# Attention and a gated causal convolution on one core: the depthwise convolution in quarter-array matmuls

## The chip, the cores and the metric

The kernel runs on one core of a Trainium2 chip. A core has five engines that run their own instruction streams and wait for one another by semaphores: TensorE (PE, matmuls and transposes, with a separate row PEld for weight loads), VectorE (DVE), ScalarE (ACT), GpSimd (POOL) and SyncE (SP, which here only issues DMAs). A name with a q behind it, such as SPq, is an engine's issuing side. Matmuls write to PSUM, which has eight banks; everything else works in SBUF. The metric is the device time of one execution in microseconds (us). Three runs of the kernel before took 227.63, 227.98 and 228.9 us; the median is 227.98.

## The reference

```python
# q, k, v: (8, 8, 576, 64): batch, heads, sequence, head width
scores = matmul(q, k.T) / sqrt(64)
scores = where(row // 64 >= col // 64, scores, -1e9)       # causal by blocks of 64
attn   = exp(scores - max); attn = attn / (sum(attn) + 1e-9)
x      = matmul(attn, v) -> (8, 576, 512)                  # heads side by side
# w_val, w_out: (512, 512); conv_w: (5, 512)
gate_pre = sum over k of conv_w[k] * (x shifted down by 4 - k rows)
gate     = 1 / (1 + exp(-gate_pre))
out      = ((gate * (x @ w_val)) @ w_out)                  # (8, 576, 512), float32
```

All 512 features of the convolution are independent: each has its own five weights, and no feature mixes with another. The multiplication by `w_val` and `w_out` mixes them.

## The kernel before

The work is cut into 32 pairs of heads: pair `p` is batch `b = p // 4` and feature chunk `g = p % 4`, 128 features. One loop over `p` (with 12 iterations more to drain it) writes the instructions of all engines in the order in which they run; no scheduler changes it. Each engine takes its own instructions in that order. One iteration `p` issues, on PE:

1. `s_tile(p, 0)` and `s_tile(p, 1)`: score matmuls. The two heads of a pair lie on the partitions 0 to 63 and 64 to 127, so these matmuls use 64 rows of the array and 128 columns (`64*128` in the profile). ACT takes the exponentials from PSUM (`pt`), POOL zeroes the masked corners.
2. `av(p - 1)`: 30 matmuls of the pair before, with 65 columns streamed (64 values and a column of ones for the sum). DVE divides by the sum (`rc`, `x`).
3. `s_tile(p, 2)`.
4. `conv(p - 2)`: the convolution of one feature chunk. For every tap `kk` there is a diagonal 128x128 matrix `DG[:, g, kk, :]` with the tap's weights, and the chunk of `x`, features on partitions, is streamed through it at an offset of `kk` columns. Five taps add up in PSUM, once for each half of the 576 rows (`hf`): ten matmuls of 288 columns. ACT then takes `tanh` of half the sum (`th`), for sigmoid(z) = (1 + tanh(z / 2)) / 2.
5. `trans(p + 2)`: eight transposes of the queries and keys that are needed two iterations later, and every fourth iteration four more for the last 64 rows (`trans_tails`, "tails" below). POOL has cast them to 16 bits before.
6. `s_tile(p, 3)`: two small score matmuls.
7. `val(p - 5)`: 128 output features of `x @ w_val`, two halves of four matmuls of 288 columns; DVE multiplies by `th + 1` and writes `gv` (`w_val` was scaled by 0.5 when it was cast).
8. `xtrans(p - 1)`: five transposes of the attention's result into `xts`, features on partitions.
9. `out_tile`: in most later iterations one, at times two: four matmuls of 512 columns with `gv` as weights and `w_out` streamed. DVE copies the result out and SP stores it.

All but the scores use four PSUM banks, `G0` to `G3`, in turn: `g1()` takes the next, `g2()` the next two. A step waits until whoever read its bank last is done: DVE for most, ACT for the banks of `conv`. With no tails an iteration takes nine banks, so `val`'s second half gets the first bank of `conv`, and `xtrans` the second.

SP issues the loads of `q`, `k` (four iterations ahead) and `v` (three ahead) and the stores in one queue, in program order. ACT issues the loads of the weights at the start. `weights(s)` in iterations 0 to 5 prepares them: the loads and the transposed taps `convT` in 0, the diagonals `DG` on DVE in 1 (20 operations), the casts of `w_val` on ACT in 2 and 3 and of `w_out` in 4 and 5.

All matmuls that are no transposes are issued by the helper `mm` at L33, so the profile shows them under that line; they are told apart by the tiles: `G<-xt,DG` is the convolution, `G<-v,pt` the attention's second product, `G<-xt,w_val` the projection, `G<-w_out,gv` the output.

Of the kernel before, what the change touches and what calls it, by code (L numbers as in the profile page):

```python
# [10 lines left out]
def kernel(  # L11
# [10 lines left out]
    nc = tc.nc  # L22
    fp32 = mybir.dt.float32
    fp16 = mybir.dt.float16
# [31 lines left out]
    convT = const([128, 4, 5], fp32, "convT")  # L56
    DG = const([128, 4, 5, 128], fp16, "DG")

# [176 lines left out]

    def conv(p):
        b, g = divmod(p, 4)
        r = g2()
        for hf in range(2):
            for kk in range(5):  # L240
                mm(G[0:128, (r + hf) % 4, 0:288], DG[0:128, g, kk, 0:128],
                   xts[b % NX][0:128, g, kk + 288 * hf:kk + 288 * hf + 288],
                   start=(kk == 0), stop=(kk == 4))
        t = p4.tile([128, 2, 288], fp32, tag="th", name="th")
        th[p] = t
        for hf in range(2):
            nc.scalar.activation(out=t[0:128, hf, 0:288], in_=G[0:128, (r + hf) % 4, 0:288],  # L247
                                 func=AF.Tanh, bias=0.0, scale=0.5)

    def val(p):  # L250
        b, g = divmod(p, 4)
        r = g2()
        for hf in range(2):
            for fc in range(4):
                mm(G[0:128, (r + hf) % 4, 0:288], w_val_sb[0:128, fc, 128 * g:128 * g + 128],
                   xts[b % NX][0:128, fc, 4 + 288 * hf:4 + 288 * hf + 288],
                   start=(fc == 0), stop=(fc == 3))
# [3 lines left out]
        t = th.pop(p)  # L261
        for hf in range(2):
            nc.vector.scalar_tensor_tensor(  # L263
                out=gv[u][0:128, g, bi, hf, 0:288], in0=t[0:128, hf, 0:288], scalar=1.0,
                in1=G[0:128, (r + hf) % 4, 0:288], op0=ALU.add, op1=ALU.mult)

# [43 lines left out]
    def weights(s):  # L310
        if s == 0:
            nc.scalar.dma_start(out=w_st[0:128],
                                in_=moe_w_val.rearrange("(fc p) n -> p fc n", p=128))
            nc.scalar.dma_start(out=w_st2[0:128],
                                in_=moe_w_out.rearrange("(fc p) n -> p fc n", p=128))
            r = g1()
# [6 lines left out]
        elif s == 1:  # L323
            for g in range(4):
                for kk in range(5):
                    nc.vector.tensor_scalar(out=DG[0:128, g, kk, 0:128], in0=ident16[0:128],
                                            scalar1=convT[0:128, g, kk:kk + 1], scalar2=None,
                                            op0=ALU.mult)
        elif s in (2, 3):
            a = 2 * (s - 2)  # L330
            nc.scalar.activation(out=w_val_sb[0:128, a:a + 2, 0:512],
                                 in_=w_st[0:128, a:a + 2, 0:512],
                                 func=AF.Copy, bias=0.0, scale=0.5)
        elif s in (4, 5):
            a = 2 * (s - 4)
            nc.scalar.activation(out=w_out_sb[0:128, a:a + 2, 0:512],
                                 in_=w_st2[0:128, a:a + 2, 0:512],
                                 func=AF.Copy, bias=0.0, scale=1.0)

    outs = []  # L340
    for p in range(NP + 12):
# [13 lines left out]
        if p < NP:  # L355
# [16 lines left out]
        if 0 <= p - 5 < NP:  # L372
            val(p - 5)
        if 0 <= p - 1 < NP:
# [41 lines left out]
```

## Time and profile before

| what | us |
|---|---|
| median of three runs | 227.98 |
| the profiled execution, as timed | 228.03 |
| its span, first to last instruction | 226.2 |
| PE busy | 206.6 |
| PEld busy | 148.1 |
| DVE busy | 136.0 |
| ACT busy | 124.7 |
| POOL busy | 84.7 |
| convolution matmuls, 320 of 287 ns | 44.9 busy |
| tanh, 64 of 437 ns | 23.7 busy |
| projection matmuls, 256 of 287 ns | 36.6 busy |

Times in the profile are us from the start of the span unless marked ns. A matmul's record runs from its start to a modelled end, and the next may start long before that; so a group's busy time is the union of its records, and the pace of PE is seen from starts, not from the mean length. In a row of a timeline the first number is the start, the second the length of the merged stretch, and the count stands behind the x; what stands in brackets is the engine's idle time before it and what ended it. The mean granted clock of PE was 0.985 of full speed.

### The profile page before, as it was taken

The page shows a single profiled execution, that of the slowest core. Times are in us where ns is not written, and L with a number is a line of the kernel's source. Part 1 is how long each engine was busy: PE and PEld are TensorE (multiplying, and loading weights), DVE is VectorE, ACT ScalarE, POOL GpSimd, SP SyncE. Part 2 cuts the span into 40 slices and gives each one's busy share as a digit, 9 for nine tenths or more (in the row PEclk, how much of TensorE's full clock was granted, in tenths as well). Part 3 has the DMA queues.
Part 4 walks back from the last instruction along what each step waited for, and adds up shares of the span by engine and source line. Part 5 has one row for each costly group of instructions (what it writes and reads, how often), then busy time and mean ns, then how long its engine had stood idle before and what let it go on. Part 6 is the DMA issues. An engine that isn't in the chain of part 4 may idle for free.

```text
span 226.2 us, 6996 instructions
## 1 busy us (share of the span) xinstructions
PE 206.6 (91%) x2712; PEld 148.1 (65%) x2712; DVE 136.0 (60%) x326; ACT 124.7 (55%) x197; POOL 84.7 (37%) x224
## 2 busy tenths in 40 slices
PE   0494599999999999999999999999999999999993
PEld 0363387777777776677777776776777776767661
DVE  1228245556666766666666667666666666656683
ACT  2055189977755554566666554555666665563100
POOL 1380465454534343544434333544454332220000
PEclk9999589999999999999999999999999999999999
DMA  5999997978888968987689767977888762111226
GB/s 131 214 235 330 199 203 169 206 154 187 187 193 207 228 147 205 245 200 190 164 187 227 175 173 173 231 188 188 198 194 206 174 159 96 46 49 46 96 93 232
DMA packets 120715, 40.32 MB, mean 178 GB/s; under 512 B 115045, under 2 KB 115045, under 8 KB 120682
## 3 DMA queue, kind: packets, MB, share of 16 engines
q1 hardware_dynamic: 119616, 37.77, 69.4%
q10 hardware_dynamic: 1066, 2.11, 2.8%
q8 instruction: 21, 0.34, 0.7%
q14 instruction: 12, 0.10, 0.2%
HBM read 30.42 MB, written 9.44 MB: 176 GB/s over the span
## 4 chain that ended last, share of the span: by engine, by line
PE 83%; SPq 5%; DMA 4%; ACT 2%; issue 2%; DVE 1%; POOL 0%; POOLq 0%; DVEq 0%; ACTq 0%
PE G L33 60%; PE S L33 13%; PE G L155 6%; DMA qkst<-in_k_dram 4%; PE G L228 4%; SPq L107 3%; ACT pt L186 1%; SPq L115 1%; PE G L142 1%; ACT th L247 1%; SPq L118 1%; POOL qk L131 0%; DVE rc L218 0%; SPq L96 0%; DVE osb L274 0%
## 5 line engine op out<-in xcount | busy, mean ns | idle before, releaser
L186 ACT ACTIVATE pt<-S 128x1024 f16<-128x1024 f32 (+1 forms) x128 | 101.1, 841 | 80.3 <-PE S L33 79.4
L160 DVE COPY qkT<-G 128x1024 f16<-128x1024 f16 x32 | 22.1, 692 | 45.2 <-PE G L155 45.2
L193 POOL MEMSET pt<- 64x128 f16 x96 | 17.2, 199 | 74.3 <-ACT pt L186 73.8
L33 PE MATMUL G<-xt,DG 128*128 128x288 f16 x320 | 44.9, 287 | 0.0
L131 POOL CAST qk<-qkst 128x1024 f16<-128x1024 f32 x31 | 32.4, 1045 | 21.3 <-DMA qkst<-in_k_dram 19.0
L33 PEld LDWEIGHTS <-pt 128*128 128x128 f16 x960 | 32.4, 99 | 7.2 <-issue 6.5
L33 PE MATMUL G<-xt,w_val 128*128 128x288 f16 x256 | 36.6, 287 | 0.0
L33 PE MATMUL G<-v,pt 128*128 128x65 f16 x960 | 36.2, 197 | 0.0
L33 PE MATMUL G<-w_out,gv 128*128 128x512 f16 x144 | 35.5, 379 | 0.0
L33 PEld LDWEIGHTS <-DG 128*128 128x128 f16 x320 | 28.6, 97 | 8.5
L155 PE MATMUL G<-ident,qk 128*128 128x128 f16 x256 | 21.2, 230 | 14.0 <-POOL qk L131 8.1
L263 DVE SCALAR_TENSOR_TENSOR gv<-th,G 128x288 f16<-128x288 f32 x64 | 29.0, 454 | 6.7 <-PE G L33 4.7
L219 DVE TENSOR_TENSOR x<-G,rc 128x320 f16<-128x320 f32 x64 | 31.5, 492 | 2.2
L274 DVE COPY osb<-G 128x512 f32<-128x512 f32 x36 | 24.9, 692 | 10.5 <-PE G L33 10.4
L33 PE MATMUL S<-qkT 64*128 64x512 f16 (+3 forms) x256 | 30.5, 313 | 0.8 <-ACT pt L186 0.6
L155 PEld LDWEIGHTS <-qk 128*128 128x128 f16 x256 | 17.9, 103 | 16.0 <-POOL qk L131 8.6
L33 PEld LDWEIGHTS <-qkT 64*128 64x128 f16 x512 | 16.4, 96 | 18.2 <-issue 12.4
L247 ACT ACTIVATE th<-G 128x288 f32<-128x288 f32 x64 | 23.7, 437 | 6.7 <-PE G L33 6.7
L33 PEld LDWEIGHTS <-w_val 128*128 128x128 f16 x256 | 22.8, 98 | 6.3
L134 POOL CAST v<-vst 128x640 f16<-128x640 f32 x32 | 23.2, 725 | 2.2 <-POOL pt L195 0.3
L218 DVE RECIPROCAL rc<-G 128x5 f32<-128x5 f32 x64 | 12.2, 190 | 15.2 <-PE G L33 14.3
L33 PEld LDWEIGHTS <-gv 128*128 128x128 f16 x144 | 13.0, 98 | 10.7
(33 smaller groups left out, 96.8 us busy)
## 6 DMA issues: line engine op xcount, KB each, us to landing
out_dram<-osb SPq DMA_DIRECT2D x36, 256.0 KB, 2.2
qkst<-in_q_dram SPq DMA_DIRECT2D x64, 128.0 KB, 3.0
qkst<-in_k_dram SPq DMA_DIRECT2D x64, 128.0 KB, 3.2
vst<-in_v_dram SPq DMA_DIRECT2D x64, 128.0 KB, 3.3
tlst<-in_q_dram SPq DMA_DIRECT2D x8, 128.0 KB, 3.5
tlst<-in_k_dram SPq DMA_DIRECT2D x8, 128.0 KB, 4.1
vst<-in_v_dram SPq DMA_DIRECT2D x32, 32.0 KB, 2.7
w_st<-in_moe_w_val_dram ACTq DMA_DIRECT2D x1, 1024.0 KB, 6.0
```

Of the source, the lines that this page charges most:

```text
L33: nc.tensor.matmul(out=out, lhsT=lhsT, rhs=rhs, start=start, stop=stop, skip_group_check=True)
L131: eng.tensor_copy(out=t[0:128], in_=s[0:128])
L134: nc.gpsimd.tensor_copy(out=v16s[p % NV][0:128, 0:5, 0:2, 0:64], in_=vsts[p % NVS][0:128, 0:5, 0:2, 0:64])
L155: nc.tensor.transpose(out=r[:, o:o + 128], in_=t[0:128, i, c, 0:2, 0:64], identity=ident16[0:128, 0:128])
L160: nc.vector.tensor_copy(out=o[0:128], in_=r.rearrange("p (i s) -> p i s", i=2))
L186: nc.scalar.activation(out=pts[p % NPT][0:128, 0:2, 512 * t:512 * t + n], in_=s[0:128, 0:2, 0:n], func=AF.Exp, bias=0.0, scale=0.125)
L193: nc.gpsimd.memset(pt[64:128, 0:2, o:o + 64], 0.0)
L218: nc.vector.reciprocal(out=rc[0:128], in_=O[:, :, 64:65])
L219: nc.vector.tensor_tensor(out=x[0:128, 0:5, h, 0:64], in0=O[:, :, 0:64], in1=rc[0:128].to_broadcast([128, 5, 64]), op=ALU.mult)
L247: nc.scalar.activation(out=t[0:128, hf, 0:288], in_=G[0:128, (r + hf) % 4, 0:288], func=AF.Tanh, bias=0.0, scale=0.5)
L263: nc.vector.scalar_tensor_tensor(out=gv[u][0:128, g, bi, hf, 0:288], in0=t[0:128, hf, 0:288], scalar=1.0, in1=G[0:128, (r + hf) % 4, 0:288 ...
L274: nc.vector.tensor_copy(out=o[0:128], in_=G[0:128, r, 0:512])
```

## The change

The convolution is computed in quarters of the array. A unit is now two feature chunks (`c2`: chunks 0 and 1, or 2 and 3) and one half of the rows (`hf`), where it was one chunk and both halves. A chunk's 128 features lie on two halves of the partitions (`row` 0 and 1). For every tap four matmuls of 64x64 are issued: chunk `2 * c2 + col`, feature half `row`, each with the 64x64 diagonal block of its features, since the rest of the diagonal matrix is zero. The result of (`row`, `col`) goes to bank `row` of the unit's two and to the partitions of `col`. A unit has 20 matmuls of 288 columns, in the order (0,0), (1,1), (0,1), (1,0) within a tap, and there are 32 units as before; each unit still gives two banks to two `tanh` operations.

So the features come out in another order: the 128 partitions of a result hold one half of each of two chunks. To match, the columns of `w_val` are permuted when they are cast (four ACT operations of half the size instead of two), and the rows of `w_out` when they are loaded (four DMAs of 64 partitions instead of one of 128). The diagonals `DG` hold only 64 columns, and DVE makes them in 40 operations of 64x64. Since a unit needs two chunks, it is issued one iteration later: `p - 3` instead of `p - 2`; iterations 3 to 34 hold one each, where 2 to 33 did.

```diff
-    DG = const([128, 4, 5, 128], fp16, "DG")
+    DG = const([128, 4, 5, 64], fp16, "DG")
...
-    def conv(p):
-        b, g = divmod(p, 4)
+    def conv(b, c2, hf):
         r = g2()
-        for hf in range(2):
-            for kk in range(5):
-                mm(G[0:128, (r + hf) % 4, 0:288], DG[0:128, g, kk, 0:128],
-                   xts[b % NX][0:128, g, kk + 288 * hf:kk + 288 * hf + 288],
+        t = th.get((b, c2))
+        if t is None:
+            t = th[(b, c2)] = p4.tile([128, 2, 2, 288], fp32, tag="th", name="th")
+        for kk in range(5):
+            for rc in ((0, 0), (1, 1), (0, 1), (1, 0)):
+                row, col = rc
+                g = 2 * c2 + col
+                rs, cs = slice(64 * row, 64 * row + 64), slice(64 * col, 64 * col + 64)
+                mm(GT[(r + row) % 4][cs, 0:288], DG[rs, g, kk, 0:64],
+                   xts[b % NX][rs, g, kk + 288 * hf:kk + 288 * hf + 288],
                    start=(kk == 0), stop=(kk == 4))
-        for hf in range(2):
-            nc.scalar.activation(out=t[0:128, hf, 0:288], in_=G[0:128, (r + hf) % 4, 0:288],
+        for row in range(2):
+            nc.scalar.activation(out=t[0:128, row, hf, 0:288],
+                                 in_=GT[(r + row) % 4][0:128, 0:288],
                                  func=AF.Tanh, bias=0.0, scale=0.5)
...
-    def val(p):
-        b, g = divmod(p, 4)
+    def val(b, x):
+        c2, row = divmod(x, 2)
...
-            nc.scalar.dma_start(out=w_st2[0:128],
-                                in_=moe_w_out.rearrange("(fc p) n -> p fc n", p=128))
+            for col in range(2):
+                for x in range(2):
+                    nc.scalar.dma_start(
+                        out=w_st2[64 * col:64 * col + 64].rearrange(
+                            "p (a x) n -> p a x n", a=2)[:, :, x],
+                        in_=moe_w_out.rearrange("(a c x i) n -> c x i a n",
+                                                a=2, c=2, x=2)[col, x])
...
-                    nc.vector.tensor_scalar(out=DG[0:128, g, kk, 0:128], in0=ident16[0:128],
-                                            scalar1=convT[0:128, g, kk:kk + 1], scalar2=None,
-                                            op0=ALU.mult)
+                    for hh in range(2):
+                        hs = slice(64 * hh, 64 * hh + 64)
+                        nc.vector.tensor_scalar(out=DG[hs, g, kk, 0:64],
+                                                in0=ident16[hs, 64 * hh:64 * hh + 64],
+                                                scalar1=convT[hs, g, kk:kk + 1], scalar2=None,
+                                                op0=ALU.mult)
         elif s in (2, 3):
             a = 2 * (s - 2)
-            nc.scalar.activation(out=w_val_sb[0:128, a:a + 2, 0:512],
-                                 in_=w_st[0:128, a:a + 2, 0:512],
-                                 func=AF.Copy, bias=0.0, scale=0.5)
+            for x in (a, a + 1):
+                nc.scalar.activation(
+                    out=w_val_sb[0:128, 0:4, 128 * x:128 * x + 128].rearrange(
+                        "p f (c i) -> p f c i", c=2),
+                    in_=w_st[0:128].rearrange("p f (a c r i) -> p f a r c i",
+                                              a=2, c=2, r=2)[:, :, x // 2, x % 2],
+                    func=AF.Copy, bias=0.0, scale=0.5)
...
-        if 0 <= p - 2 < NP:
-            conv(p - 2)
+        if 0 <= p - 3 < NP:
+            bq, un = divmod(p - 3, 4)
+            conv(bq, un // 2, un % 2)
...
-            val(p - 5)
+            val(*divmod(p - 5, 4))
```

On PE, in the middle of the loop, where the convolution stands between the third score tile and the transposes of `q` and `k`, the kernel before has this order (`qkT` and `kt` are transposed queries and keys, `qk16` those to be transposed, G0 to G3 the four banks):

```order
L33 LDWEIGHTS qkT_2062
L33 MATMUL S_2276<-kt_0_99,qkT_2062 128x64
L33 LDWEIGHTS DG_86
L33 MATMUL G3_107<-xt_0_101,DG_86 128x288 [waits DVE_49]
L33 LDWEIGHTS DG_86
L33 MATMUL G3_107<-xt_0_101,DG_86 128x288
...
L33 MATMUL G0_104<-xt_0_101,DG_86 128x288 [waits DVE_49]
...
L155 LDWEIGHTS qk16_2166 [waits Pool_49]
L155 MATMUL G1_105<-ident16_79,qk16_2166 128x128 [waits DVE_49]
```

And the changed kernel, at the same place:

```order
L33 LDWEIGHTS qkT_1925
L33 MATMUL S_2151<-kt_1_100,qkT_1925 128x64
L33 LDWEIGHTS DG_86
L33 MATMUL G3_107<-xt_0_101,DG_86 64x288 [waits DVE_49]
L33 LDWEIGHTS DG_86
L33 MATMUL G0_104<-xt_0_101,DG_86 64x288 [waits DVE_49]
L33 LDWEIGHTS DG_86
L33 MATMUL G3_107<-xt_0_101,DG_86 64x288
...
L155 LDWEIGHTS qk16_2027 [waits Pool_49]
L155 MATMUL G1_105<-ident16_79,qk16_2027 128x128 [waits DVE_49]
```

The block lies between the same neighbours. It alternates between its two banks at every matmul, where it filled one after the other, and both are complete only at its end.

On ACT, in the first iterations, the difference is this (`w_st_83` is where the weights `w_out` land, `pt` the exponentials):

```order
 L186 ACTIVATE pt_96<-S 128x2x512 x2
-L312 DMA w_st<-in_moe_w_val_dram 128x4x512
-L314 DMA w_st_83<-in_moe_w_out_dram 128x4x512
+L319 DMA w_st<-in_moe_w_val_dram 128x4x512
+L323 DMA w_st_83<-in_moe_w_out_dram 64x2x512 x4
 L186 ACTIVATE pt_96<-S 128x2x512
```

```order
 L186 ACTIVATE pt_98<-S 128x2x512 x2
-L331 ACTIVATE w_val<-w_st 128x1024
+L347 ACTIVATE w_val<-w_st 128x4x128 x2
 L186 ACTIVATE pt_98<-S 128x2x512
-L247 ACTIVATE th<-G_107 128x288
-L247 ACTIVATE th<-G_104 128x288
 L186 ACTIVATE pt_98<-S 128x2x64
```

Three DMA issues more stand ahead of the third exponential of iteration 0; in iteration 2 the cast of `w_val` is two operations, and the pair of `tanh` has moved to the next iteration.

More of the change, by code (lines that the diff above doesn't have):

```diff
@@ L254, in val @@
             for fc in range(4):
[L255 removed]
+                mm(GT[(r + hf) % 4][0:128, 0:288],
+                   w_val_sb[0:128, fc, 128 * x:128 * x + 128],
                    xts[b % NX][0:128, fc, 4 + 288 * hf:4 + 288 * hf + 288],
@@ L260, in val @@
             gv[u] = p2.tile([128, 4, 2, 2, 288], fp16, tag="gv", name="gv")
-        t = th.pop(p)
+        t = th[(b, c2)]
         for hf in range(2):
             nc.vector.scalar_tensor_tensor(
-                out=gv[u][0:128, g, bi, hf, 0:288], in0=t[0:128, hf, 0:288], scalar=1.0,
-                in1=G[0:128, (r + hf) % 4, 0:288], op0=ALU.add, op1=ALU.mult)
+                out=gv[u][0:128, x, bi, hf, 0:288], in0=t[0:128, row, hf, 0:288], scalar=1.0,
+                in1=GT[(r + hf) % 4][0:128, 0:288], op0=ALU.add, op1=ALU.mult)
+        if row == 1:
+            th.pop((b, c2))
     def out_tile(u, t):
```

2 lines of the change are left out of this document (removed).

## The prediction

> **What bounds the kernel now.** First the page: busy time, the slices, and the chain that ended last.
>
> ```profile
> span 226.2 us, 6996 instructions
> PE 206.6 (91%) x2712; PEld 148.1 (65%) x2712; DVE 136.0 (60%) x326; ACT 124.7 (55%) x197; POOL 84.7 (37%) x224
> PE   0494599999999999999999999999999999999993
> PE 83%; SPq 5%; DMA 4%; ACT 2%; issue 2%; DVE 1%; POOL 0%; POOLq 0%; DVEq 0%; ACTq 0%
> ```
>
> PE has gaps in the first six slices and hardly any after; 83% of the chain is PE. Matmuls are pipelined, so a busy PE alone proves little. I therefore read the windows, cut at the starts of loop iterations (each begins with the first score matmul): one iteration in the middle, the start-up iterations 2 to 5, the long stretch of iterations 6 to 28, and one with much DMA.
>
> ```profile
> 101.84:107.89 6.05, 6.05 (x86) 4.35 (x85) 3.94 (x9) 3.74 (x6) 2.45 (x6) 1.00 0.79 191
> 27.21:47.29 20.08, 19.55 (x298) 14.84 (x298) 10.49 (x27) 18.27 (x28) 10.51 (x25) 0.94 0.92 190
> 47.29:188.92 141.63, 141.39 (x1940) 102.00 (x1939) 92.84 (x215) 86.02 (x138) 60.78 (x145) 1.00 0.79 189
> 119.98:126.26 6.28, 6.28 (x90) 4.57 (x89) 4.21 (x10) 3.74 (x6) 2.45 (x6) 1.00 0.96 230
> ```
>
> The columns are length, then busy PE, PEld, DVE, ACT and POOL, the clock, the DMA share and GB/s. PE fills the long stretch at full clock, ACT and DVE have some 2 us free in each 6.05 us. Next, PE's order inside that iteration; here the **starts** matter, since a record's length includes its pipeline's end.
>
> ```profile
> 101.84 0.61 PE L33 MATMUL S<-qkT 64*128 64x512 f16 x6
> 102.38 1.09 PE L33 MATMUL G<-v,pt 128*128 128x65 f16 x30
> 103.40 0.28 PE L33 MATMUL S<-qkT 64*128 64x256 f16 x2
> 103.52 0.29 PE L33 MATMUL S<-kt,qkT 64*128 64x64 f16 x8
> 103.74 1.40 PE L33 MATMUL G<-xt,DG 128*128 128x288 f16 x10
> 104.98 0.61 PE L155 MATMUL G<-ident,qk 128*128 128x128 f16 x8
> 105.52 0.20 PE L33 MATMUL S<-kt 64*128 64x64 f16 x2
> 105.66 1.15 PE L33 MATMUL G<-xt,w_val 128*128 128x288 f16 x8
> 106.65 0.44 PE L228 MATMUL G<-ident,x 128*128 128x128 f16 x5
> 106.93 1.03 PE L33 MATMUL G<-w_out,gv 128*128 128x512 f16 x4
> 107.89 0.39 PE L33 MATMUL S<-qkT 64*128 64x512 f16 x2
> ```
>
> No step waits for another engine, so time taken from PE here is taken from the end. The convolution (DG) holds PE from 103.74 to 104.98: 1.24 us, ten matmuls at 0.124 us.
>
> **The change, part by part.** *Streaming.* A block's ten full-array matmuls become 20 quarter-array ones of the same 288 columns, in five groups of four. If four run at once, a block streams for 5 x 0.124 = 0.62 us. The trace has no matmul of fewer than 128 output columns, but it has half-height ones:
>
> ```profile
> L33 PE MATMUL S<-qkT 64*128 64x512 f16 x64 | 13.1, 407 | 0.1
> ```
>
> 32 pairs cover 13.1 us, 0.409 us a pair, and one alone lasts 0.407: the two heads, on the upper and the lower rows, run together. Quarters also split the columns, which this does not show. Bounds for a group of four: 0.124 us (all together) and 0.248 us (only the two row halves together). I take 0.124, by that nearest row.
>
> *Dispatch and first loads.* 20 load-and-matmul pairs per block need no more issue than the attention rows show: 30 pairs from 102.38 to 103.40, 0.034 us each, with the turn in array shape behind them in it; four are then at most 0.136 us, so issue about keeps pace. At a block's start the four weight loads may come one after another: 0 to 3 x 0.034 = 0.10 us; I take 0.05.
>
> *Turning the array's shape.* Eight transposes, followed once by full-array work (tails) and in the iteration above by half-height work:
>
> ```profile
> 98.71 0.61 PE L155 MATMUL G<-ident,qk 128*128 128x128 f16 x8
> 99.15 0.39 PE L142 MATMUL G<-ident,tl 128*128 128x128 f16 x4
> 196.87 1.40 PE L33 MATMUL G<-xt,DG 128*128 128x288 f16 x10
> 198.20 0.20 PE L33 MATMUL S<-kt 64*128 64x64 f16 x2
> ```
>
> 0.44 us there, 0.54 above (104.98 to 105.52); the convolution likewise takes 1.24 before transposes and 1.33 (196.87 to 198.20) before half-height work: a change of shape costs 0.10 us. Today the turn lies ahead of the convolution (behind the half-height scores). A quarter-array block keeps it and adds one behind. Bounds 0 and 0.2; I take 0.10.
>
> So a block costs 0.62 + 0.05 + 0.10 = 0.77 us for 1.24: 0.47 saved (0.41 to 0.52 by these last two bounds).
>
> *Where that counts.* Blocks move one iteration later, from 2-33 to 3-34. Iterations 6 to 29 are PE's: 24 x 0.47 = 11.3 us. In 30 and 31 the turn exists already (the 1.33 row): 2 x 0.56 = 1.1. In the tail everything around is full-array:
>
> ```profile
> 206.99 1.40 PE L33 MATMUL G<-xt,DG 128*128 128x288 f16 x10
> 208.22 1.14 PE L33 MATMUL G<-xt,w_val 128*128 128x288 f16 x8
> ```
>
> There 1.23 becomes 0.87 (a turn on both sides), twice, and a third block of 0.87 is added: -0.15. In iterations 2 to 5 PE would lose 4 x 1.24 - 3 x 0.77 = 2.65 us, but ACT is busy 18.27 of 20.08 us there:
>
> ```profile
> 35.01 1.06 ACT L331 ACTIVATE w_val<-w_st 128x1024 f16<-128x1024 f32 x1
> 102.33 2.86 ACT L186 ACTIVATE pt<-S 128x1024 f16<-128x1024 f32 x3 [2.27 <-PE S L33]
> 105.06 0.73 ACT L247 ACTIVATE th<-G 128x288 f32<-128x288 f32 x2
> 105.83 0.28 ACT L186 ACTIVATE pt<-S 128x128 f16<-128x128 f32 x1
> ```
>
> ACT loses one pair of tanh there (0.73), and each weight cast of 1.06 becomes two of half the width: by 0.95 for 1024 columns (2.86 / 3) and 0.28 for 128, half is about 0.57, so +0.1 for each of two casts. ACT's floor is 18.27 - 0.73 + 0.2 = 17.7, so 0.3 to 2.3 us may be won; I take 1.0.
>
> *Start-up pieces at nothing.* DVE's 20 diagonals become 40 of 64x64, and the w_out load becomes four issues on ACT's queue:
>
> ```profile
> 17.09 3.33 DVE L326 TENSOR_SCALAR DG<-ident,convT 128x128 f16<-128x128 f16 x20
> 21.19 0.49 DVE L219 TENSOR_TENSOR x<-G,rc 128x320 f16<-128x320 f32 x1
> 25.43 1.04 PE L155 MATMUL G<-ident,qk 128*128 128x128 f16 x8 [5.71 <-POOL qk L131]
> 13.81 0.37 ACTq L314 DMA_DIRECT2D w_st<-in_moe_w_out_dram  x1
> ```
>
> The diagonals cost between nothing more and 3.3 us (0.17 each again). The attention rows queued behind them on DVE end at 21.7 and are wanted after the transposes of 25.43 to 26.4, so 4.7 us cover them; without cover PE would stand up to 3.3 us. Three issues more, 1.1 us, sit ahead of ACT's third exponential at 14.95, inside that same wait for the q/k cast. Uncovered: 1.1 us.
>
> *What is late next.* The projection's second half reuses the convolution's first PSUM bank, freed by the first tanh. That ends 3.6 us into the iteration (105.06 + 0.4 - 101.84), since ACT runs its exponentials first. The second half starts now at 4.3 (105.66 + 0.5 - 101.84), then at 3.8: just free. Every fourth iteration has tails in the ring, and there the first half wants that bank, 3.82 + 0.22 (four transposes of 0.055) - 0.47 = 3.57 us in: some 0.07 us, six times, 0.4 us lost.
>
> Sum: 11.3 + 1.1 - 0.15 + 1.0 - 0.4 = 12.9 us. The profiled execution took 228.03 us (226.2 span and 1.8 around it), the median is 227.98: **215.1 us**.
>
> **Rivals.**
>
> *The weight loads bind (229 us).* Four loads must fit behind 0.124 us of streaming. For f16 loads of 128 columns the rows never show the load binding. The one slow load row is f32, at start-up:
>
> ```profile
> L33 PE MATMUL G<-ident,conv_nat 5*128 5x5 f32 x8 | 1.9, 353 | 0.0
> 10.57 1.03 PE L155 MATMUL G<-ident,qk 128*128 128x128 f16 x8 [1.89 <-POOL qk L131]
> 11.54 1.04 PE L33 MATMUL S<-qkT 64*128 64x512 f16 x6
> ```
>
> Eight loads with five-column matmuls take 1.9 us, (1.9 - 0.353) / 7 = 0.22 us from one to the next, nearly all load. Half the columns and half the bytes make 0.055 us: one after another 0.22 us a group, not 0.124. A block is then 4 x 0.22 + 3 x 0.055 + 0.124 + 0.10 = 1.27 us: 24 x 0.03 = 0.7 lost, 1.6 more in the tail with its third block, 0.1 won in 30 and 31, 0.8 at the start; 228.0 + 1.4. Against it: eight transposes took 0.97 us there (10.57 to 11.54) and 0.44 later, so PE ran at half its later pace; at full pace four loads are 0.11 us and hide. Chance 0.14.
>
> The Trainium skill says in "TensorEngine Tiling (Array Packing)", section "Restrictions", that column tiling disables the fast weight load. By "TensorE: Matmul & The Clock Gate", section "LDWEIGHTS", a load takes columns / 1.2 ns, an estimated 0.053 us for 64, and by that alone the time would be this rival's; whether the four overlap no row here can say.
>
> *Columns take turns (233 us, slower).* If the two column halves of one row half cannot stream together, a group needs two passes: 1.24 + 0.05 + 0.10 = 1.39 us a block, 0.15 worse in 24 iterations (3.6), 0.1 in 30 and 31, 2.0 in the tail, 0.5 won at the start: 228.0 + 5.2. It decides as soon as a group exceeds 0.22 us. For it: no matmul here splits columns. Against: the row halves do overlap. Chance 0.12.
>
> The Trainium skill ("TensorE: Matmul & The Clock Gate", "Measured speedup vs the span model") reports 10.6x for 16 row-and-column tiles, which speaks against this rival; no run here shows it.
>
> *The loads of q, k, v become the bound (226 us).* The same bytes in a shorter loop need a DMA share of 0.79 x 6.05 / 5.58 = 0.86. If 0.79 were the ceiling, the long stretch would not shrink: about 2 us remain. Against: one iteration ran at 0.96 and 230 GB/s, and SP stands idle behind output copies:
>
> ```profile
> SPq L275 <- DVE osb L274: 38.8, 23, 5.6
> ```
>
> That is 38.8 us of the span in which the queue that issues the loads waited for a result to store. Chance 0.06.
>
> **How the numbers follow.** Forecast 0.68, rivals 0.14, 0.12, 0.06. The forecast alone spans 212 to 219: 0.52 a block and 2.3 at the start below; above, 0.3 at the start and groups of 0.16 us. The range goes on to 228.5, over the DMA case and the half-hidden loads, leaving out the column case: 211.5 to 228.5. Measurement tells 0.5% (1.1 us) from no change; faster takes the forecast, the DMA case and a third of the load case (loads half hidden): 0.79; same another third: 0.05; slower the last and the column case: 0.16.
>
> **What would show it.** Right: DG matmuls start in fours within about 0.1 us, a block starts 0.75 to 0.80 us ahead of the next step, iterations take 5.6 us, PE still fills the stretch. Wrong: groups 0.22 us or more apart; a turn well over 0.10 us; new idle time of PE ahead of the projection (on tanh) or the transposes (on the q/k cast).

## The result and the profile after

The changed kernel took **220.41 us** (median of 4 runs, 220.09 to 220.96), beside 228.31 for the kernel before (4 runs, 227.63 to 228.9): a ratio of 0.966, interval 0.962 to 0.970, so 7.9 us faster. The forecast was 215.1 us, 12.9 us faster. The profiled execution took 220.65 us. Medians and ranges below are over all runs of a kernel, while ratios and intervals leave out runs more than 1.5% above its fastest.

The page of the changed kernel: busy time, PE's slices, and the chain that ended last.

```profile
span 218.8 us, 7669 instructions
PE 191.7 (88%) x3032; PEld 133.6 (61%) x3032; DVE 144.0 (66%) x346; ACT 122.2 (56%) x199; POOL 85.1 (39%) x224
PE   0390569889889999999999999999999999999993
PE 68%; DVE 9%; DMA 5%; SPq 4%; issue 4%; ACT 4%; POOL 3%; POOLq 0%; ACTq 0%; DVEq 0%
```

PE lost 14.9 us of busy time, but the span lost only 7.4. DVE, 1% of the chain before, now holds 9%: something new on DVE sets the end for a while, and PE's empty slices say it is at the start. The fourth slice, 16 to 22 us, stands at 0 where it was 4.

The windows of the changed kernel, cut at iteration starts like those of before: a middle iteration, iterations 2 to 5, and iterations 9 to 28.

```profile
102.41:107.96 5.55, 5.55 (x94) 3.86 (x94) 3.94 (x9) 3.63 (x6) 2.45 (x6) 1.00 0.87 212
30.50:49.63 19.13, 17.39 (x319) 13.08 (x318) 10.59 (x28) 17.73 (x28) 10.42 (x25) 0.91 0.79 172
67.49:183.01 115.52, 115.11 (x1895) 80.11 (x1894) 82.53 (x188) 72.64 (x120) 52.76 (x126) 1.00 0.85 205
```

The same twenty iterations 9 to 28 of the kernel before:

```profile
64.23:188.92 124.69, 124.69 (x1694) 89.27 (x1694) 82.19 (x188) 74.80 (x120) 51.77 (x125) 1.00 0.79 190
```

9.17 us are saved there, 0.46 an iteration, and the DMA share went from 0.79 to 0.85 without stopping anything. Now PE's order in the middle iteration of the changed kernel:

```profile
104.09 0.29 PE L33 MATMUL S<-kt,qkT 64*128 64x64 f16 x8
104.31 0.81 PE L33 MATMUL G<-xt,DG 64*64 64x288 f16 x20
105.05 0.62 PE L155 MATMUL G<-ident,qk 128*128 128x128 f16 x8
105.60 0.20 PE L33 MATMUL S<-kt 64*128 64x64 f16 x2
105.73 1.15 PE L33 MATMUL G<-xt,w_val 128*128 128x288 f16 x8
```

The block holds PE from 104.31 to 105.05: 0.74 us, where it was 1.24. The single records inside such a block start at 98.391, .394, .397 and .401 us, then at 98.538 to .548, then every 0.123 us in fours. A group of four takes as long as one full matmul did. The weight loads are in the groups of instructions:

```profile
L33 PE MATMUL G<-xt,DG 64*64 64x288 f16 x640 | 25.9, 287 | 0.0
L33 PEld LDWEIGHTS <-DG 64*64 64x64 f16 x640 | 15.8, 105 | 3.0 <-issue 0.8
```

640 loads of 105 ns each cover only 15.8 us: 0.099 us for four (15.8 / 160), less than a group's 0.123. By these records the loads overlap one another and the streaming.

So the block does what was forecast. Where the other 5 us went shows when both traces are cut at the same iteration starts (each is the first score matmul of its iteration):

| part | before, us | after, us | gained | forecast |
|---|---|---|---|---|
| to iteration 0 | 11.54 | 11.82 | -0.28 | 0 |
| iterations 0 and 1 | 15.67 | 18.68 | **-3.01** | 0 |
| iterations 2 to 5 | 20.08 | 19.13 | 0.95 | 1.0 |
| iterations 6 to 8 | 16.94 | 17.86 | **-0.92** | 1.4 |
| iterations 9 to 29 | 130.74 | 121.07 | 9.67 | 9.5 |
| iterations 30, 31 and the tail | 31.23 | 30.24 | 0.99 | 0.95 |
| span | 226.2 | 218.8 | 7.4 | 12.9 |

(Forecast per row: 0.47 us an iteration; the 0.4 for the tanh wait is put to 9 to 29.) Two rows fail, both early. First, iterations 0 and 1 of the changed kernel, on DVE, ACT and PE:

```profile
17.38 11.30 DVE L340 TENSOR_SCALAR DG<-ident,convT 64x64 f16<-64x64 f16 x40
28.70 0.20 DVE L218 RECIPROCAL rc<-G 128x5 f32<-128x5 f32 x1
14.06 9.10 ACTq L323 DMA_DIRECT2D w_st<-in_moe_w_out_dram  x4
23.21 1.19 ACT L186 ACTIVATE pt<-S 128x1024 f16<-128x1024 f32 x2 [8.80 <-DMA vst<-in_v_dram]
24.28 1.04 PE L33 MATMUL S<-qkT 64*128 64x512 f16 x6 [7.38 <-ACT pt L186]
30.11 0.45 PE L228 MATMUL G<-ident,x 128*128 128x128 f16 x5 [1.80 <-DVE x L219]
```

The 40 diagonals last 11.30 us instead of 3.33, so the attention rows behind them start at 28.70 instead of 20.34, and PE waits 1.80 us for their result at 30.11. The four `w_out` issues occupy ACT's queue from 14.06 to 23.16, and the third exponential runs at 23.21 instead of 14.95; PE waits 7.38 us for it before it can write new scores.

Second, iterations 6 to 8, on PE and POOL:

```profile
58.75 0.62 PE L155 MATMUL G<-ident,qk 128*128 128x128 f16 x8 [0.81 <-POOL qk L131]
64.57 0.62 PE L155 MATMUL G<-ident,qk 128*128 128x128 f16 x8 [1.05 <-POOL qk L131]
63.47 1.04 POOL L131 CAST qk<-qkst 128x1024 f16<-128x1024 f32 x1 [3.29 <-DMA qkst<-in_k_dram]
```

PE waits for the q/k cast, and the cast waited for the load of `k`: the loads are late, at 60 us, for something that happened much earlier. The stretch from 18 to 29 us, in the kernel before and in the changed one:

```profile
18.00:29.00 11.00, 5.29 (x72) 3.92 (x70) 4.76 (x21) 3.46 (x6) 2.91 (x7) 0.72 1.11 251
```

```profile
18.00:29.00 11.00, 4.03 (x56) 3.00 (x55) 10.39 (x40) 4.32 (x6) 2.73 (x7) 1.00 1.23 200
```

The DMA engines were busier (1.23 for 1.11) and moved less (200 GB/s for 251). The share adds up the times of all packets, so it passes 1 where packets overlap. Counted by queue from the packet records of the traces, 1.05 MB of weights arrive in this stretch in both kernels; but SP's queue, with `q`, `k` and `v`, moves 1.15 MB in the changed kernel and 1.69 in the one before, at 27 ns a packet and 21. The queue of the weight loads, before and after:

```profile
q10 hardware_dynamic: 1066, 2.11, 2.8%
```

```profile
q10 hardware_dynamic: 1114, 2.11, 4.1%
```

The same 2.11 MB took 143.5 us of DMA engine time (4.1% of 16 x 218.8) instead of 101.3 (2.8% of 16 x 226.2): 129 ns a packet for 95. The difference is 2.6 us on all 16 engines, near what is missing in iterations 6 to 8 (0.92 + 1.4 = 2.3); by itself that proves nothing, since packet times overlap.

### The profile page after: what moved, and what is told of

It reads as the page before. It is cut to its first block, busy times and chain, and to the rows that moved or that the text cites. A ratio compares the mean times of both kernels' runs of the same rounds, so it can differ in the third digit from the quotient of the medians.

```text
span 218.8 us, 7669 instructions
## 1 busy us (share of the span) xinstructions
PE 191.7 (88%) x3032; PEld 133.6 (61%) x3032; DVE 144.0 (66%) x346; ACT 122.2 (56%) x199; POOL 85.1 (39%) x224
## 3 DMA queue, kind: packets, MB, share of 16 engines
q10 hardware_dynamic: 1114, 2.11, 4.1%
## 4 chain that ended last, share of the span: by engine, by line
PE 68%; DVE 9%; DMA 5%; SPq 4%; issue 4%; ACT 4%; POOL 3%; POOLq 0%; ACTq 0%; DVEq 0%
PE G L33 48%; PE S L33 11%; PE G L155 6%; DVE DG L340 5%; DMA qkst<-in_k_dram 4%; PE G L228 4%; SPq L107 2%; DVE x L219 2%; DMA vst<-in_v_dram 2%; ACT th L250 2%; ACT pt L186 2%; POOL qk L131 1%; DVE rc L218 1%; SPq L115 1%; DVE qkT L160 1%
## 5 line engine op out<-in xcount | busy, mean ns | idle before, releaser
L131 POOL CAST qk<-qkst 128x1024 f16<-128x1024 f32 x31 | 32.4, 1044 | 24.4 <-DMA qkst<-in_k_dram 17.9
L155 PEld LDWEIGHTS <-qk 128*128 128x128 f16 x256 | 15.7, 103 | 17.5 <-DVE qk L131 6.2
L33 PE MATMUL G<-xt,DG 64*64 64x288 f16 x640 | 25.9, 287 | 0.0
L218 DVE RECIPROCAL rc<-G 128x5 f32<-128x5 f32 x64 | 12.2, 190 | 15.9 <-PE G L33 15.8
L33 PEld LDWEIGHTS <-gv 128*128 128x128 f16 x144 | 13.0, 98 | 10.7
L33 PEld LDWEIGHTS <-DG 64*64 64x64 f16 x640 | 15.8, 105 | 3.0 <-issue 0.8
```

The lines of the kernel that those rows point to most:

```text
L33: nc.tensor.matmul(out=out, lhsT=lhsT, rhs=rhs, start=start, stop=stop, skip_group_check=True)
L131: eng.tensor_copy(out=t[0:128], in_=s[0:128])
L155: nc.tensor.transpose(out=r[:, o:o + 128], in_=t[0:128, i, c, 0:2, 0:64], identity=ident16[0:128, 0:128])
L218: nc.vector.reciprocal(out=rc[0:128], in_=O[:, :, 64:65])
```

## The experiments

Three suspects are left: the diagonals, ACT's blocked queue, and the slow, late loads. The first four kernels take them apart.

**One load of `w_out` again.** Its rows then come unpermuted, so the output is not the reference's; everything else stays.

```diff
-            for col in range(2):
-                for x in range(2):
-                    nc.scalar.dma_start(
...
+            nc.scalar.dma_start(out=w_st2[0:128],
+                                in_=moe_w_out.rearrange("(fc p) n -> p fc n", p=128))
```

> The changed kernel with the w_out load as one DMA of 128 partitions again, as in the kernel before (the rows of w_out are then not permuted, so the output is not the reference's; all engines do the same work). Theory A, the start-up cost sits on two engines: the four-part load blocks ACT's queue for 9 us and its slower packets push the q/k/v loads back, which PE pays in iterations 6 to 8; the 40 diagonals on DVE, 11.3 us, hold back the first attention rows. Undoing the load alone: ACT's third exponential starts near 15 us again, but the diagonals still end near 28.5 us, so iteration 2 still begins near 30 us; the waits of PE on the q/k cast in iterations 6 to 8 (2.3 us) go. About 218 us. Theory B, the shorter loop itself asks for more than the DMA gives: the waits in 6 to 8 stay, 220 us. Theory C, the load is the whole loss: iteration 2 begins near 27 us, 215 us.

Measured: 218.19 us (218.15 to 218.64), ratio 0.956, interval 0.952 to 0.960. ACT and DVE of this kernel:

```profile
15.11 1.02 ACT L186 ACTIVATE pt<-S 128x1024 f16<-128x1024 f32 x1 [0.82 <-PE S L33]
17.26 11.27 DVE L335 TENSOR_SCALAR DG<-ident,convT 64x64 f16<-64x64 f16 x40
```

The third exponential is back at 15.11, iteration 1 starts at 16.59, and the waits of iterations 6 to 8 are gone: iteration 9 starts at 65.15 instead of 67.49. But iteration 2 starts at 30.61, no earlier than in the changed kernel (30.50), because the diagonals alone now hold it. So the load costs 2.2 us while the slow diagonals stand beside it, through the late loads rather than through ACT's block.

**The diagonals by halves.** The same 40 operations in another order: all on partitions 0 to 63 first, then all on 64 to 127.

```diff
-            for g in range(4):
-                for kk in range(5):
-                    for hh in range(2):
-                        hs = slice(64 * hh, 64 * hh + 64)
+            for hh in range(2):
+                hs = slice(64 * hh, 64 * hh + 64)
+                for g in range(4):
+                    for kk in range(5):
```

> The changed kernel with the same 40 diagonal operations on DVE in another order: all 20 of the lower 64 partitions, then all 20 of the upper, instead of alternating. If it is the alternation between partition halves that makes one cost 0.28 us, they fall to 0.10 to 0.17 us each, 4 to 6.6 us in all, and the attention rows behind them run at 21.5 to 24 us. If it is the operation count or the 64-partition shape, they stay at 11.3 us. By theory A ACT is still blocked by the load until 23 us, iteration 1 still begins near 24.3 us, iteration 2 near 29 instead of 30.5, and the late loads remain: 218.5 to 220 us. By the theory that the diagonals are the whole loss: 215 us.

Measured: 219.58 us (219.41 to 220.02), ratio 0.962, interval 0.959 to 0.965. The group of diagonals in the changed kernel, and in this one, with its row in the timeline:

```profile
L340 DVE TENSOR_SCALAR DG<-ident,convT 64x64 f16<-64x64 f16 x40 | 10.7, 268 | 0.6
```

```profile
L340 DVE TENSOR_SCALAR DG<-ident,convT 64x64 f16<-64x64 f16 x40 | 6.1, 262 | 0.0
17.30 6.15 DVE L340 TENSOR_SCALAR DG<-ident,convT 64x64 f16<-64x64 f16 x40
```

One operation lasts the same (268 and 262 ns), but the group covers 6.1 us instead of 10.7: in this order the records overlap, 0.154 us from start to start (6.15 / 40), and where halves alternate they don't, 0.283 (11.30 / 40). It is the alternation that costs, not the count. In the time it is worth 0.8 us here, since ACT is still blocked (third exponential at 23.03) and the loads are still late (iteration 8 takes 6.85 us).

The Trainium skill ("VectorE: DVE Perf Modes", "Two Vector instructions with no wait between them") has a model for this: an instruction whose output or input starts in another group of 32 partitions than the last one's is held until every earlier Vector instruction has finished. Both numbers agree with it; it gives no price, and 0.13 us an operation is what it cost here.

**Both together**, the two edits above in one kernel (its output is not the reference's either).

> Both together (again with the rows of w_out not permuted). Theory A: neither cause alone explains the start; with both gone iteration 2 begins near 27 us as in the kernel before, the waits in 6 to 8 go, and the forecast's sum is reached: 214.5 to 216 us. Theory B (the shorter loop outruns the loads whatever the start): iteration 2 near 27 us, but 2 to 3 us of waits on the q/k cast reappear a few iterations later: 217 to 218 us.

Measured: 216.42 us (215.49, 216.06, 216.78 and 219.24), ratio 0.947, interval 0.942 to 0.951; span 214.3. That is a little above the 214.5 to 216 expected. PE's only long wait at the start is then the one that the kernel before had:

```profile
25.64 1.03 PE L155 MATMUL G<-ident,qk 128*128 128x128 f16 x8 [5.40 <-POOL qk L131]
```

Together the two cost 4.0 us (220.41 - 216.42; 4.4 by 216.06, the median of the three runs that lie close). They cover each other in part: the diagonals are worth 1.8 us with the load mended and 0.8 without, the load 3.2 with the diagonals mended and 2.2 without. Iterations 0 and 1 take 15.54 us again (15.67 before). Of the 0.96 us by which its profiled execution (216.06) is above the forecast, 0.72 is a wait for a q/k cast at 60.10, in iteration 8.

**Four loads of full height.** The kernel above loads `w_out` once. This one issues four DMAs again, but each over all 128 partitions, one chunk each (rows unpermuted, output not the reference's), so that count and shape come apart. Beside the kernel with the halves it differs in one thing more, the order in which rows are read.

```diff
+            for fc in range(4):
+                nc.scalar.dma_start(out=w_st2[0:128, fc],
+                                    in_=moe_w_out[128 * fc:128 * fc + 128, :])
```

> Beside the run with both causes undone (216.4 us): the same kernel with the w_out load in four DMAs again, but each over all 128 partitions (one per feature chunk; the rows are not permuted, so the output is not the reference's). In the built program every DMA issue waits for an earlier DMA that used the same one of eight semaphores, on whichever queue. Number theory: it is the count of issues on ACT that blocks ACT, since each waits for a q/k/v load to land: ACT's third exponential starts near 23 us again, iteration 1 near 24, 218 to 219.5 us. Shape theory: it is the 64 partitions that slow the packets (140 to 200 ns instead of 85 to 100) and so the landing: with 128 the third exponential starts near 16 to 18 us and the time stays at 216 to 217 us.

Measured: 216.81 us (216.64 to 217.93), ratio 0.947, interval 0.942 to 0.952, beside 219.58 for the same kernel with four half-height loads: 2.8 us (the kernel before took 229.14 beside the one, 228.37 beside the other). ACT, the load queue and the DMA window:

```profile
13.69 7.94 ACTq L322 DMA_DIRECT2D w_st<-in_moe_w_out_dram  x4
21.68 1.19 ACT L186 ACTIVATE pt<-S 128x1024 f16<-128x1024 f32 x2 [7.46 <-DMA qkst<-in_k_dram]
```

```profile
q10 hardware_dynamic: 1114, 2.11, 3.1%
```

```profile
18.00:29.00 11.00, 6.25 (x101) 4.83 (x102) 8.69 (x43) 5.58 (x8) 4.17 (x9) 1.00 1.09 250
```

ACT is blocked all the same, 7.94 us for four issues. But the weights take 3.1% of the engines' time again, and 250 GB/s flow in the window; SP's queue moves 1.68 MB in it at 20 ns a packet, where it moves 1.18 MB at 28 ns in the same kernel with half-height loads. So four issues block ACT whatever their shape, and that cost 0.4 us by the medians (216.81 against 216.42), which is within the scatter of these runs. The half-height shape makes the packets slow on both queues, and that costs 2.8. Here PE paid most of it at once: with full-height loads iteration 6 starts at 46.18 instead of 48.54, and iterations 6 to 8 still take 17.48 us (17.71 with the halves).

Why do the issues take so long? In the built program's order on ACT each of them waits for a semaphore, and so do most of the loads on SP, for the same eight (DMAHW0 to 7). The changed kernel:

```
L319 DMA w_st<-in_moe_w_val_dram 128x4x512 [waits DMAHW5_49]
L323 DMA w_st_83<-in_moe_w_out_dram 64x2x512 [waits DMAHW2_49]
L323 DMA w_st_83<-in_moe_w_out_dram 64x2x512 [waits DMAHW5_49]
L323 DMA w_st_83<-in_moe_w_out_dram 64x2x512 [waits DMAHW0_49]
L323 DMA w_st_83<-in_moe_w_out_dram 64x2x512 [waits DMAHW3_49]
```

The program hands the eight out in turn, so a DMA waits until the eighth before it, of either queue, has landed; the second of the four waits on the semaphore that the `w_val` load just took. The trace bears this out: the landings that the four wait for come at 14.04, 18.78, 21.25 and 22.54 us, and the issues start 0.02 us behind each, at 14.06, 18.80, 21.27 and 22.56. One issue itself lasts 0.60 to 0.69 us (0.34 to 0.51 at full height, 0.37 in the kernel before); the rest of the 9.1 us is this waiting. No run changed the semaphores.

**Late loads, stacked diagonals.** This kernel has the reference's result again. The diagonals are 20 operations of 128x64, from an identity of 64 columns laid twice on top of itself; the four half-height loads are spread over iterations 2 to 5, their casts move to 6 and 7.

```diff
+                nc.vector.tensor_copy(out=id2[hs], in_=ident16[hs, 64 * hh:64 * hh + 64])
...
+                    nc.vector.tensor_scalar(out=DG[0:128, g, kk, 0:64], in0=id2[0:128],
+                                            scalar1=convT[0:128, g, kk:kk + 1], scalar2=None,
+                                            op0=ALU.mult)
-        elif s in (4, 5):
-            a = 2 * (s - 4)
+        if s in (2, 3, 4, 5):
+            col, x = divmod(s - 2, 2)
+            nc.scalar.dma_start(
...
+        if s in (6, 7):
+            a = 2 * (s - 6)
```

> A kernel that computes the reference with both causes removed another way: the diagonals as 20 operations of 128x64 from two stacked 64x64 identities (two copies more), and the four parts of the w_out load issued one each in iterations 2 to 5 on ACT's queue, its casts in 6 and 7. Theory A: diagonals 3 to 3.4 us, no long ACT wait, the megabyte of w_out comes out of a later phase in which the DMA has less slack than none in 12 to 30 us: iteration 2 begins near 25 to 26 us, since the q/k loads have the DMA to themselves earlier; 213 to 215 us. Theory B: the w_out parts then collide with the q/k loads in iterations 3 to 6 and PE waits there: 216 to 218 us.

Measured: 215.64 us (215.14 to 217.28), ratio 0.946, interval 0.941 to 0.951. Diagonals, PE's waits and two windows:

```profile
17.23 3.01 DVE L335 TENSOR_SCALAR DG<-id,convT 128x64 f16<-128x64 f16 x20
32.56 0.62 PE L156 MATMUL G<-ident,qk 128*128 128x128 f16 x8 [1.55 <-POOL qk L132]
42.92 0.62 PE L156 MATMUL G<-ident,qk 128*128 128x128 f16 x8 [1.57 <-POOL qk L132]
```

```profile
24.00:36.00 12.00, 9.54 (x204) 7.66 (x206) 6.21 (x17) 10.50 (x17) 5.41 (x13) 0.95 1.07 216
36.00:48.00 12.00, 9.09 (x186) 6.70 (x179) 5.83 (x15) 8.13 (x14) 5.90 (x14) 1.00 0.99 218
```

The diagonals take 3.01 us, and iteration 2 starts at 23.05, 4.4 us earlier than with both edits above (27.42). Yet iteration 8 starts at 56.47, against 56.67 there: PE waits for the q/k casts in iterations 3 to 5, and the DMA share is 1.07 and 0.99. The time lies between the two theories' ranges, and the waits are those of the second. In this kernel the loads set the pace for the first 55 us; what was won ahead of them is waited for again.

**Fewer turns of the array.** Two kernels, both on top of the last one, test the 0.10 us for a change of shape. The first puts the fourth score tile, half-height, directly behind the convolution; the second puts the convolution directly behind the attention product and all half-height scores behind the convolution.

```diff
             conv(bq, un // 2, un % 2)
+        if p < NP:
+            s_tile(p, 3)
...
-        if p < NP:
-            s_tile(p, 3)
```

> The kernel with late w_out parts and stacked identities (215.6 us) with one step moved: the fourth score tile (two half-height matmuls) directly behind the convolution instead of behind the q/k transposes. Turn theory (each change of the array's shape costs PE 0.10 us): an iteration has six turns instead of seven, 0.10 us off some 24 iterations that PE sets: 2.4 us, less up to 0.1 us more of waiting on tanh in every fourth iteration (0.7 us): 213 to 214 us. If the turns overlap with something or the wait on tanh grows in all iterations: no change, 215.6 us.

```diff
             av(p - 1)
+        if 0 <= p - 3 < NP:
+            bq, un = divmod(p - 3, 4)
+            conv(bq, un // 2, un % 2)
         if p < NP:
             s_tile(p, 2)
+            s_tile(p, 3)
...
-        if 0 <= p - 3 < NP:
-            bq, un = divmod(p - 3, 4)
-            conv(bq, un // 2, un % 2)
...
-        if p < NP:
-            s_tile(p, 3)
```

> The same kernel with the convolution moved ahead of the third score tile, directly behind the attention product, and the fourth score tile directly behind the third. Turn theory: five turns instead of seven, 0.2 us off some 24 iterations (4.8 us), and tanh comes 1 us earlier, so the waits of the projection on tanh (0.15 us every fourth iteration) go as well: 209.5 to 211 us. If ACT's order then binds (tanh ahead of the third exponential, which the next iteration's first score tile waits for): iterations of 5.5 us as before and 215 us.

Measured: 215.01 us (212.98 to 215.91; ratio 0.936, 0.928 to 0.944) and **212.8** us (211.83 to 214.56; ratio 0.929, 0.923 to 0.936). Neither total comes down to what the turns alone would give (213 to 214 and 209.5 to 211). A middle iteration takes 5.56 us in the changed kernel, 5.45 with the one turn removed and 5.34 with two: 0.11 us a turn. PE in the second one:

```profile
104.12 0.81 PE L33 MATMUL G<-xt,DG 64*64 64x288 f16 x20
104.86 0.28 PE L33 MATMUL S<-qkT 64*128 64x256 f16 x2
104.98 0.28 PE L33 MATMUL S<-kt,qkT 64*128 64x64 f16 x8
105.10 0.19 PE L33 MATMUL S<-kt 64*128 64x64 f16 x2
105.22 0.62 PE L156 MATMUL G<-ident,qk 128*128 128x128 f16 x8
105.68 1.14 PE L33 MATMUL G<-xt,w_val 128*128 128x288 f16 x8
```

The convolution is 0.74 us still; the turns are gone from the steps around it: from the transposes to the next step 0.46 instead of 0.55, from the scores of 64 columns to the next 0.12 instead of 0.22. In the first of the two the saving is not resolved in the total: a 3.04 us wait for a q/k cast stands in its iteration 5, and the iterations with tails, which wait for the tanh, stay at 5.92. The second has no tanh wait, and its tails iterations take 5.56. Its profiled execution was its longest, 214.56 us; in it PE waits four times behind 100 us for a cast of queries and keys, 0.27 to 1.21 us each, which the changed kernel does not do there:

```profile
122.87 0.62 PE L156 MATMUL G<-ident,qk 128*128 128x128 f16 x8 [1.21 <-POOL qk L132]
```

Those casts wait for loads, so at 5.34 us an iteration the loads are no longer always in time. The profile of the repeat below, of another of the longer executions (214.14), has such waits too, 0.31 to 1.26 us. Whether the faster executions have them no profile shows.

**Loads later still.** The second kernel with the `w_out` loads in iterations 6 to 9, and no output tile before iteration 12.

```diff
-        if s in (2, 3, 4, 5):
+        if s in (6, 7, 8, 9):
...
-        n = 1 if (len(outs) < 5 and p < NP) else 2
+        n = 0 if p < 12 else 1 if (len(outs) < 5 and p < NP) else 2
```

> The kernel with the convolution behind the attention product (212.8 us), its four w_out parts issued in iterations 6 to 9 instead of 2 to 5, the casts in 10 and 11, and no output tile before iteration 12. Theory that the loads set the first 55 us (DMA share about 1 there): a megabyte less of some nine by iteration 8 brings iteration 8 from 57.7 to about 54 us; the postponed output tiles and the megabyte come back where PE sets the pace: 209.5 to 211.5 us. Theory that in this faster loop the loads are short of the DMA everywhere: what is won at the start is waited for later, 212 to 213 us.

> The kernel with the convolution behind the attention product once more, beside the one above: 211.8 to 213.4 us, with iterations of 5.34 us in the middle.

Measured: 212.43 us (211.8 to 213.94; ratio 0.932, 0.927 to 0.936), and the kernel it builds on, run again beside it, 213.2 (209.93, 212.26, 214.14 and 214.82; the ratio 0.924, 0.917 to 0.931, rests on the first two). Iteration 8 starts earlier, at 54.12 instead of 57.69 (56.81 in the repeat), and PE then waits, for instance here:

```profile
58.70 0.62 PE L156 MATMUL G<-ident,qk 128*128 128x128 f16 x8 [1.85 <-POOL qk L132]
69.38 0.62 PE L156 MATMUL G<-ident,qk 128*128 128x128 f16 x8 [1.67 <-POOL qk L132]
```

No difference that these runs resolve, as the second theory had it: the lead of 3.57 us at iteration 8 is down to 0.97 at iteration 18 (112.26 against 113.23), with one postponed output tile, 0.86 us, still to be made up. The best version stays the convolution-first kernel, 15.5 to 16.3 us under the kernel before in its two measurements, and 7.6 under the change as it was (212.8 against 220.41).

## Why the prediction was right, and where it was wrong

The block and the long stretch came as worked out; the start did not. The 220.41 us lies inside the stated range, 211.5 to 228.5, but above the 212 to 219 of the forecast itself: the range was stretched over the DMA case and half-hidden loads, and neither happened, while nothing in the sum or the range stood for the 4 us that the start-up cost. That the time fell inside is in part luck. Two sums in the working are off, though the forecast does not hang on them: bounds of 0 to 0.10 and 0 to 0.2 give 0.32 to 0.62 saved a block, not 0.41 to 0.52, and the upper end, with groups of 0.16 us (24 x 0.18) and 0.7 less at the start, is 220.1 and not 219.

The signs named beforehand were mixed. Groups start in fours within 0.01 us, iterations take 5.56 us, PE fills the stretch, and the block, 0.74, is just under its 0.75 to 0.80. But PE has the new idle time that was to show an error: ahead of the transposes in iterations 6 to 8, and by 0.15 us ahead of the projection where there are tails.

**The block, right.** "0.62 + 0.05 + 0.10 = 0.77" measured 0.74. The trace has 0.147 us for the first group and 0.123 for each other, so first loads cost 0.02, not 0.05; the turn behind the block is 0.09 (0.214 from the last group's start to the transposes, less 0.12 of streaming). The two experiments on the order of steps set a change of shape at 0.11 us.

**"Weight loads bind", wrong.** Four loads take 0.099 us of PEld a group, and a group starts every 0.123 us, not 0.22. The page before could have lowered this rival's chance: its 960 loads `<-pt` of 99 ns each, 95 us one after another, cover 32.4 us, so load records overlapped there already. What it could not show is four loads into four quarters. The restriction that the Trainium skill names ("TensorEngine Tiling (Array Packing)", "Restrictions") is thus no bar to a load of 64x64 hiding behind 288 columns; nothing here tells whether the fast load was off.

**"Columns take turns", wrong.** Four matmuls of two row halves and two column halves start within 0.01 us and their group lasts 0.123.

**"Where that counts", right from iteration 9 on.** 9.67 us against 9.5; iterations 30, 31 and the tail 0.99 against 0.95. In the tail a block was put at 0.87, with a turn on both sides. The block of the changed kernel, with full-array work around it:

```profile
198.47 1.08 PE L33 MATMUL G<-v,pt 128*128 128x65 f16 x30
199.48 0.81 PE L33 MATMUL G<-xt,DG 64*64 64x288 f16 x20
200.22 1.16 PE L33 MATMUL G<-xt,w_val 128*128 128x288 f16 x8
```

and the same attention product ahead of the block before, which started at 206.99:

```profile
206.07 1.08 PE L33 MATMUL G<-v,pt 128*128 128x65 f16 x30
```

The block takes 0.74 from its start; the turn ahead of it shows in the step before, 1.01 us to the block instead of 0.92. Together 0.83, near the 0.87.

**Iterations 2 to 5, right**: 0.95 against 1.0, with ACT busy 17.73 of 19.13 us, the floor that was worked out as 17.7. The 1.0 was picked from 0.3 to 2.3, so that it came so close is luck.

**"What is late next", right in place, too small in size.** PE of the changed kernel in an iteration with tails:

```profile
99.91 0.20 PE L33 MATMUL S<-kt 64*128 64x64 f16 x2
100.19 1.02 PE L33 MATMUL G<-xt,w_val 128*128 128x288 f16 x7
```

The projection starts 0.28 us behind the small scores, where it is 0.13 without tails (105.60 to 105.73): 0.15 us of waiting for the first tanh, which ends at 100.16, where 0.07 was forecast. Six times that is 0.9 us instead of 0.4.

**"Start-up pieces at nothing", wrong, and with it most of the missing 5 us.** Three assumptions fell:

- "0.17 each again" for the diagonals. A small operation was taken to pipeline like a large one; halves in turn cost 0.283 each, 11.3 us in all. The cover of 4.7 us was right and was simply exceeded. Measured price: 0.8 to 1.8 us.
- "Three issues more, 1.1 us". They were costed as 0.37 us like the one issue that the trace showed. The four last 0.60 to 0.69 each and wait for earlier loads in between, so they hold ACT 9.1 us. By the four full-height loads this alone cost 0.4 us, within the scatter.
- That the load moves the same bytes in the same time. Nothing in the sum stood for the DMA engines; the half-height packets put the loads of `q`, `k` and `v` behind. In the changed kernel, where the slow diagonals hid it at first, PE paid for it 30 us later, in iterations 6 to 8. Measured price of the load in all: 2.2 to 3.2 us, and of its shape 2.8.

Together 4.0 us, and 216.42 without them, 1.3 above the forecast (medians; 1.0 by 216.06).

**"The loads of q, k, v become the bound"** was a rival for the long stretch, and there it didn't happen: the share is 0.85 to 0.87, as the 0.86 of its sum, with no wait. It was true in the first 60 us, where it was not looked for: the stretch from 18 to 29 us had a share of 1.11 in the kernel before already.

## What to carry to other kernels

Quarter-array matmuls with a weight load each ran four at a time here and cut a block-diagonal product from 1.24 to 0.74 us; order the work so that steps of one array shape stand together, which gave 0.11 us for each change of shape removed. What the main loop wins is easily lost in preparation: an operation cut into partition halves is a new kind of operation on DVE and in the DMA engines, so cost it as unknown, not as the old row halved, and keep the halves apart or stack them. And price a transfer on the stream that shares the DMA engines with it, not on the step that issues it: here the bill came as waits for other loads, up to 30 us later.

## What the runs showed of the hardware that was not expected

- DVE operations of 64x64 that alternate between partitions 0 to 63 and 64 to 127 start 0.283 us apart; the same 40 with each half together 0.154; 20 of 128x64 0.151 (3.01 / 20); 20 of 128x128 0.167 (3.33 / 20). For blocks this small the size hardly counts; the order does.
- A load of 1 MB in four DMAs over 64 partitions each took 129 ns a packet as the mean of its queue, over 128 partitions 96 ns (3.1% of 16 x 215.0 us, 1114 packets), at the same number of packets; the loads of `q`, `k` and `v` beside them took 27 to 28 ns a packet for 20. The Trainium skill says of transfers to disjoint partition halves, in "DMA: Bandwidth & Descriptors", "Rules for kernel authors": "Use one 128-partition transfer". The runs agree, 2.8 us worth. When the half-height loads were spread over four iterations the queue's share fell to 3.0% (3.5% in the convolution-first kernel), so the price belongs to half-height loads in a crowd; why is open.
- A burst of DMA issues on ACT's queue blocked ACT for 7.9 to 9.1 us, whatever the shape of the transfers: each issue started 0.02 us behind the landing of an earlier load whose semaphore the program had given it.
- Four 64x64 weight loads for every 0.123 us of streaming, each for a single matmul, cost PE nothing: records of 105 ns that together cover 0.099 us a group.
